# Pre-norm attention and gated feed-forward on one core: the maxima's product, the zero rows, and the order of values, first products and layer norms

## The chip, the cores and the metric

The kernel runs on one core of one Trainium2 chip. A core has five engines with an instruction queue each, which they work through in order: TensorE (PE in the profile; its weight loads are PEld), VectorE (DVE), ScalarE (ACT), GpSimd (POOL) and SyncE (SP), which here issues every DMA. Matrix products are written to PSUM, which has eight banks of 128 x 512 fp32 values; operands lie in SBUF, with 128 partitions. The metric is the device time of one execution in microseconds (us).

## The reference

One transformer block on 2048 tokens of width 448, in fp32. The parts that matter:

```python
def _A_ref(x, wqkv, wo):
    B, S, D = x.shape
    H = 16; Dh = D // H; W = 256
    qkv = (x @ wqkv).reshape(B, S, 3, H, Dh).transpose(2, 0, 3, 1, 4)
    q, k, v = qkv[0], qkv[1], qkv[2]
    scores = jnp.einsum("bhqd,bhkd->bhqk", q, k) * (Dh ** -0.5)
    mask = (idx[:, None] - idx[None, :] >= 0) & (idx[:, None] - idx[None, :] < W)
    scores = jnp.where(mask[None, None], scores, -1e9)
    p = _softmax(scores, axis=-1)
    o = jnp.einsum("bhqk,bhkd->bhqd", p, v)
    return o.transpose(0, 2, 1, 3).reshape(B, S, D) @ wo
...
h = x + _A_ref(_layernorm(x), A_wqkv, A_wo)
h2 = h + _B_ref(_layernorm(h), B_w_gate, B_w_up, B_w_down)   # (gelu(x@gate) * (x@up)) @ down, 1792 wide
```

A query sees itself and the 255 tokens before it. There are 16 heads of 28 columns.

## The kernel before

**Numbers.** Operands of products are split in a high part (fp32r, rounded by an ACT copy, `to_hi`, L349) and a low part (the rest, by a DVE subtraction, `to_lo`, L352). A product x @ w is the sum of high x high, low x high and high x low: 11 matmuls (`TERMS`) for the 448 rows of the contraction, which are held as four row blocks.

**Layer norm** (`layer_norm`, L364). For each tile of 128 tokens: statistics on DVE (L369, L372), three small steps on POOL that make scale and offset (L376 to L378), the normalising copy on ACT (L382), four fp32 transposes on TensorE against `ident` (L386), and high and low parts into `xT`. There are 16 tiles in the first norm and 16 in the second.

**Attention.** It runs in 16 blocks B: two halves p of the heads, in each four chunks c of 512 tokens, in each two groups of four heads. `project` makes q and k of a group for a chunk (L526); they go to DRAM and come back re-arranged (`put`, `loads`), q into `rq`, k into `rk`. Both have two halves u, used by even and odd blocks. `values` makes v of the half (L492). In a block, `scores` (L575) computes 16 score products, and DVE takes each row's masked maximum (L579). `maxima` (L587) splits the negated maxima of four heads in high and low parts, eight columns `mhl`; TensorE turns them by a transpose (L603), and ACT writes them into rows 96 to 103 of `rq` (`put`, L605). `probs` (L642) is the product of k and q with 104 contraction rows: rows 0 to 83 hold the three parts of q and k, rows 84 to 95 are zeros, rows 96 to 103 the maxima on the q side and a 0/1 pattern that picks the head's own on the k side. So the maximum is subtracted within the product, and ACT only takes the exponential (L646). POOL cuts the triangles off (`select`, L657), TensorE multiplies by v in fp32 (`attend`, L676), the sums are turned and divided (`drain`), and `output` multiplies by wo and adds to the residual `hres` (L714, L717).

The zeros are written by POOL (`zeros`, L462, eight memsets at L469, after the first layer norms' POOL steps), the pattern by DVE (eight copies at L456).

**Feed-forward.** 56 products: 14 column groups of 128 by four token chunks. Each is 22 gate and up matmuls (L801), gelu on ACT (L810), the multiplication on DVE (L813), high and low parts, and 12 down matmuls (L820). Weights are staged in `raw` or in the memory of v and split into high and low parts (`weights`, L746). The activation buffer `ge` is one tile of its own.

**The order.** The kernel records every operation with an engine, a cost, a latency, a key and what it reads and writes (`Lists.op`, L73). A planner (`run`, L150) then plays the engines forward: at each step an engine takes, among the operations that could start about soonest, the one with the lowest key. That gives the fixed order in which each engine's queue is filled; where two operations need a PSUM bank, `allowed` (L887) says which banks a kind may have. Keys are in units of one sixteenth of a block; the feed-forward part has keys from 1000 on. DMAs have a planned place on SP in the same way. In the first 26 us of the plan `idle` (L907) fills TensorE's gaps with transposes of `ident` (L913).

Of the kernel before, what the change touches and what calls it, by code (L numbers as in the profile page):

```python
# [20 lines left out]
EPS = 1e-5  # L21
# [17 lines left out]
FFN = 1000  # L39
SPANS = {"pp", "proj", "raw", "xT", "h", "rqf", "rkf", "vm", "rec0", "rec1", "rec2"}  # L40
# [9 lines left out]
def mm(n):  # L50
    return n / 2400 + 0.0155
# [14 lines left out]
class Lists:  # L66
# [42 lines left out]
    def plan(self, allowed, idle, rounds):  # L109


        best = None
        for i in range(rounds):
            end = self.run(allowed, idle, False)
            if end is not None and (best is None or end < best[0]):
                best = (end, [o.key for o in self.ops])
            if end is None or i == rounds - 1:
                break
            self.latest(end)
        for o, key in zip(self.ops, best[1]):  # L120
            o.key = key

    def latest(self, end):


        at = {o: i for i, o in enumerate(self.order)}
        back, cand = {}, {}
        for o in self.ops:
            o.left, o.ready = len(o.users), end
            if not o.left:  # L130
                cand.setdefault(o.eng, []).append(o)
        n = len(self.ops)
        while n:
            best = None
            for e, l in cand.items():
                for o in l:
                    t = min(back.get(e, end) - o.cost, o.ready - (o.fin - o.start))
                    if best is None or (t, at[o]) > best[0]:
                        best = ((t, at[o]), o)
            (t, _), o = best  # L140
            cand[o.eng].remove(o)
            o.key = back[o.eng] = t
            n -= 1
            for d in o.deps:
                d.left -= 1
                d.ready = min(d.ready, t + d.fin - d.start - d.cost if d.eng == o.eng == "pe" else t - WAKE[o.eng])
                if not d.left:
                    cand.setdefault(d.eng, []).append(d)

    def run(self, allowed, idle, emit=True):  # L150
# [49 lines left out]
        while n:  # L200
# [5 lines left out]
            if best is None:  # L206
                return None
            t, o, got = best
            e = o.eng
            if e == "pe" and t > free["pe"] + 0.1:  # L210
                cost = idle(free["pe"], t, bank_free, emit)
                if cost:
                    free["pe"] += cost
                    continue
# [17 lines left out]
            if emit:  # L232
                o.fn()
# [16 lines left out]
def block_kernel(ctx: ExitStack, tc, x, wqk_in, wv_in, wo_in, ffn_in, out):  # L250
# [24 lines left out]
    ge = pool.tile([128, 512], F32, name="ge")  # L275

    pool.tile([128, 16], F32, name="pad")
    nhalf = pool.tile([128, 1], F32, name="nhalf")
    e8 = pool.tile([128, 8], F32, name="e8")
    bnst = [pool.tile([128, 6], F32, name=f"bnst{i}") for i in range(2)]  # L280
    bnmv = [pool.tile([128, 2], F32, name=f"bnmv{i}") for i in range(4)]
    bnve = [pool.tile([128, 3], F32, name=f"bnve{i}") for i in range(4)]
    mx = [pool.tile([128, 4], F32, name=f"mx{i}") for i in range(4)]
    mhl = [pool.tile([128, 8], F32R, name=f"mhl{i}") for i in range(3)]
# [21 lines left out]
    rq = rq_m.rearrange("p (u j t) -> p u j t", u=2, j=4)  # L306
    rk = rk_m.rearrange("p (u j t) -> p u j t", u=2, j=4)
    pp = pp_m.rearrange("p (j t) -> p j t", j=4)
    v = v_m.rearrange("p (t g h d) -> p t g h d", t=NT, g=2, h=4)
    mask = mt[:, 0:384]  # L310
    junk = [mt[:, 384 + 192 * i:576 + 192 * i].bitcast(BF) for i in range(2)]
# [7 lines left out]
    def span(name, lo, n):  # L319
        return (name, lo, lo + n)  # L320
# [24 lines left out]
    def V(t):  # L345
        return span("vm", t, 1)
# [17 lines left out]
    def layer_norm(t, key, kind):  # L364
# [3 lines left out]
        def stats():  # L368
            nc.vector.bn_stats(bnst[i2], hres[:, t, :])  # L369

        def aggr():
            nc.vector.bn_aggr(bnmv[i4], bnst[i2])  # L372

        def ve():
            mv, e = bnmv[i4], bnve[i4]
            nc.gpsimd.tensor_scalar(e[:, 0:1], mv[:, 1:2], EPS, None, op0=OP.add)  # L376
            nc.gpsimd.tensor_tensor(e[:, 1:2], e[:, 0:1], nhalf, op=OP.pow)
            nc.gpsimd.tensor_scalar(e[:, 2:3], mv[:, 0:1], e[:, 1:2], -1.0, op0=OP.mult, op1=OP.mult)  # L378

        def norm():  # L380
            e = bnve[i4]
            nc.scalar.activation(xn[i2], hres[:, t, :], AF.Identity, scale=e[:, 1:2], bias=e[:, 2:3])  # L382
# [15 lines left out]
        op("dve", 0.65, 0.63, key, stats, [HR(t)], [("bnst", i2)])  # L398
        op("dve", 0.1, 0.195, key, aggr, [("bnst", i2)], [("bnmv", i4)])
        op("pool", 1.25, 1.3, key, ve, [("bnmv", i4), "nhalf"], [("bnve", i4)], port=True, tag="ve")  # L400
        op("act", 0.54, 0.63, key, norm, [HR(t), ("bnve", i4)], [("xn", i2)])
# [7 lines left out]
    def start():  # L409
# [43 lines left out]
        op("pool", 0.85, 0.9, -30, const_pick, (), ["e8"], port=True)  # L453
        for u in range(2):
            for j in range(4):
                op("dve", 0.55, 0.54, -24 + 8 * u + 2 * j, lambda u=u, j=j: nc.vector.tensor_copy(  # L456
                    rk[96:104, u, j], e8[96:104, j:j + 1].to_broadcast([8, 768])), ["e8"], [("pick", u, j)], port=True)
# [3 lines left out]

    def zeros():  # L462

        after = [o for o in L.ops if o.tag == "ve"]
        for u in range(2):
            for m, w, n in ((rq_m, "zq", 2048), (rk_m, "zk", 3072)):
                for i in range(2):
                    op("pool", 0.1 + 0.5 * n * 0.00081, 0.15 + 0.5 * n * 0.00081, -36 + 8 * u + i,
                       lambda m=m, n=n, u=u, i=i: nc.gpsimd.memset(  # L469
                           f(m[64:96, (2 * u + i) * n // 2:(2 * u + i + 1) * n // 2]), 0.0), (), [(w, u, i)],  # L470
                       after=after)
# [15 lines left out]
    def values(p, t):  # L487
        key = 128 * p + 8 * t - (37 if t < 4 and not p else 24)
# [59 lines left out]
    def loads(B):  # L548
# [3 lines left out]
        def get(s, cc, lo, n, at, key):  # L552
# [5 lines left out]
            dma(key, 246 * n, lambda: nc.sync.dma_start(f(dst[0:3 * DH, u, :, at * 128:(at + n) * 128]), src),  # L558
# [8 lines left out]
    def scores(B, i, j):  # L567
# [6 lines left out]
        def one():  # L574
            nc.tensor.matmul(bank[b.k][:, o:384], rq[0:3 * DH, u, j, i * 128:i * 128 + 128],  # L575
                             rk[0:3 * DH, u, j, m0 * 128:(i + 3) * 128], start=True, stop=True)
# [4 lines left out]
        op("pe", mm(384 - o), 0.19 + (384 - o) / 2400, s, one, [("rq", u, i)] + [("rk", u, m) for m in range(m0, i + 3)],  # L581
# [5 lines left out]
    def maxima(B, i):  # L587
# [13 lines left out]

        def tr():
            nc.tensor.transpose(bank[b.k][0:8, 384:512], f(m), ident)  # L603

        def put():  # L605
            to_hi(rq[96:104, u, :, i * 128:i * 128 + 128],
                  bank[b.k][0:8, None, 384:512].to_broadcast([8, 4, 128]))
        op("pe", 0.11, 0.286, key, tr, [("mh", k), ("ml", k), "ident"], (), b)
# [25 lines left out]
    def probs(B, m, j, o):  # L634
# [6 lines left out]
        def one():  # L641
            nc.tensor.matmul(bank[b.k][:, 0:n], rk[0:104, u, j, m * 128:m * 128 + 128],  # L642
                             rq[0:104, u, j, lo * 128:(hi + 1) * 128], start=True, stop=True)
# [102 lines left out]
    def weights(i, key):  # L746
# [3 lines left out]
        if q:  # L750
            raw, at0, need = v_m[:, 1472 * (q - 1):1472 * q], 1472 * q, ["vfree"]
# [215 lines left out]
```

## Time and profile before

| | |
|---|---|
| median of three runs | 776.94 us (774.67 to 777.94) |
| profiled execution | 777.91 us |
| its span, first to last instruction | 775.9 us |
| mean granted TensorE clock | 0.991 |
| TensorE busy | 753.0 us, 97% |
| VectorE, ScalarE, GpSimd busy | 408.0, 332.0, 176.3 us |
| DMA | 70.48 MB, 29.5% of 16 engines on SP's queue |
| first matmul; first scores | 7.6 us; 42.7 us |
| full feed-forward products | from 372 us on, 7.47 us each |
| last matmul ends | about 770.5 us |

Busy time of TensorE counts a matmul from its start to its modelled end, and matmuls overlap: the time from one matmul's start to the next one's tells more of the rate (0.23 us for 512 columns). PEclk, the granted clock, is 1 at full speed.

### The profile page before, as it was taken

To read this page: it belongs to the slowest core of one execution; us is meant where nothing else is said; L and a number is where in the kernel's file an instruction comes from. 1 tells how busy PE (TensorE), PEld (TensorE's weight loads), DVE (VectorE), ACT (ScalarE), POOL (GpSimd) and SP (SyncE) were. 2 spreads that over 40 slices of the span, in tenths; PEclk is the share of its full clock that TensorE was granted. 3 is DMA by queue.
4 is the path that set the end of the run, shared out by engine and by line. 5 is a ranking of instruction groups with operands and counts; after the bars stand their busy time and mean duration, and the time that the engine had idled before them with its cause. 6 is when DMAs were issued, how large, how long until landed. Compare 5 with 4: busy or idle time off the path is not lost.

```text
span 775.9 us, 11718 instructions
## 1 busy us (share of the span) xinstructions
PE 753.0 (97%) x4282; PEld 622.4 (80%) x4282; DVE 408.0 (53%) x1106; ACT 332.0 (43%) x727; POOL 176.3 (23%) x283
## 2 busy tenths in 40 slices
PE   6799999999999999999999999999999999999997
PEld 5687788878878776777888888888888888888885
DVE  7887966776677879857513344222242322223232
ACT  4476857776667778686211232111231111111111
POOL 7724334244335457555000000000000000000000
PEclk9899999999999999899999999999999999999999
DMA  8697446765565465223400021000000000001111
GB/s 279 188 295 217 135 132 189 193 175 160 159 188 156 119 171 170 76 80 97 138 1 1 0 79 39 1 1 1 0 1 1 0 1 1 0 1 48 47 48 47
DMA packets 44401, 70.48 MB, mean 91 GB/s; under 512 B 3832, under 2 KB 34488, under 8 KB 44344
## 3 DMA queue, kind: packets, MB, share of 16 engines
q1 hardware_dynamic: 44344, 69.75, 29.5%
q8 instruction: 33, 0.54, 0.3%
q14 instruction: 24, 0.20, 0.1%
HBM read 44.04 MB, written 25.69 MB: 90 GB/s over the span
## 4 chain that ended last, share of the span: by engine, by line
PE 88%; DVE 4%; POOL 2%; ACT 2%; DMA 2%; issue 1%; SPq 0%; DVEq 0%; POOLq 0%; ACTq 0%
PE bank L801 35%; PE bank L820 17%; PE bank L526 9%; PE bank L642 6%; PE bank L575 5%; PE bank L676 5%; PE bank L714 5%; PE bank L492 4%; DVE mt L579 1%; PE bank L386 1%; PE bank L603 1%; DMA rk<-k 1%; POOL rk L469 1%; DMA hres<-in_x_dram 1%; DVE xT L352 1%
## 5 line engine op out<-in xcount | busy, mean ns | idle before, releaser
L813 DVE TENSOR_TENSOR ge<-bank,ge 128x512 f32<-128x512 f32 x56 | 38.7, 691 | 214.1 <-PE bank L801 212.9
L579 DVE CUSTOM_DVE_ANT_0 mt<-bank,mt 128x384 bf16<-128x384 f32 (+2 forms) x256 | 129.1, 526 | 39.3 <-PE bank L575 36.9
L646 ACT ACTIVATE pp<-bank 128x384 f32<-128x384 f32 (+2 forms) x352 | 126.7, 390 | 48.5 <-PE bank L642 41.3
L526 PE MATMUL bank<-xT,proj 128*128 128x512 f32 x308 | 106.2, 417 | 4.4 <-DVE proj L352 4.3
L349 ACT ACTIVATE proj<-ge 128x512 fp32r<-128x512 f32 x56 | 35.4, 632 | 165.8 <-DVE ge L813 165.8
L657 POOL TENSOR_SCALAR_AFFINE_SELECT pp<-pp 128x512 f32<-128x512 f32 x120 | 75.0, 638 | 132.5 <-ACT pp L646 129.8
L642 PE MATMUL bank<-rq,rk 104*128 104x384 f32 (+2 forms) x352 | 101.5, 310 | 2.1 <-ACT pp L646 1.3
L810 ACT ACTIVATE ge<-bank 128x512 f32<-128x512 f32 x56 | 33.6, 599 | 151.3 <-PE bank L801 149.7
L801 PE MATMUL bank<-xT,proj 128*128 128x512 f32 x352 | 91.1, 392 | 0.3 <-ACT pp L646 0.3
L801 PE MATMUL bank<-xT,rec 128*128 128x512 f32 x352 | 91.0, 395 | 0.0
L801 PE MATMUL bank<-xT,rk 128*128 128x512 f32 x352 | 90.1, 391 | 0.0
L575 PE MATMUL bank<-rk,rq 84*128 84x384 f32 (+2 forms) x256 | 84.6, 351 | 0.9 <-DMA rk<-k 0.3
L642 PEld LDWEIGHTS bank<-rq,rk 104*128 104x128 f32 x352 | 66.4, 192 | 20.0 <-ACT pp L646 5.7
L801 PEld LDWEIGHTS bank<-xT,rec 128*128 128x128 f32 x352 | 66.1, 188 | 13.5
L801 PEld LDWEIGHTS bank<-xT,rk 128*128 128x128 f32 x352 | 66.1, 188 | 12.4
L801 PEld LDWEIGHTS bank<-xT,proj 128*128 128x128 f32 x352 | 65.8, 188 | 12.5 <-ACT pp L646 0.4
L526 PEld LDWEIGHTS bank<-xT,proj 128*128 128x128 f32 x308 | 57.7, 196 | 12.7 <-issue 4.6
L492 PE MATMUL bank<-proj,xT 128*128 128x224 f32 x352 | 56.7, 281 | 0.2 <-DVE xT L352 0.2
L352 DVE TENSOR_TENSOR proj<-ge,proj 128x512 fp32r<-128x512 f32 x56 | 38.7, 691 | 33.6 <-ACT proj L349 33.0
L575 PEld LDWEIGHTS bank<-rk,rq 84*128 84x128 f32 x256 | 47.5, 192 | 10.5 <-DVE mx L579 3.5
L492 PEld LDWEIGHTS bank<-proj,xT 128*128 128x128 f32 x352 | 50.9, 192 | 1.7 <-issue 0.4
L714 PE MATMUL bank<-wos,ohl 128*128 128x448 f32 x192 | 50.4, 375 | 1.1 <-ACT ohl L349 0.8
(81 smaller groups left out, 1034.1 us busy)
## 6 DMA issues: line engine op xcount, KB each, us to landing
rk<-k SPq DMA_DIRECT2D x44, 336.0 KB
rq<-q SPq DMA_DIRECT2D x32, 336.0 KB
q<-proj SPq DMA_DIRECT2D x16, 448.0 KB
v<-in_ffn_dram SPq DMA_DIRECT2D x8, 736.0 KB
k<-proj SPq DMA_DIRECT2D x12, 448.0 KB
raw<-in_ffn_dram SPq DMA_DIRECT2D x6, 736.0 KB
hres<-in_x_dram SPq DMA_DIRECT2D x16, 224.0 KB
q<-proj SPq DMA_DIRECT2D x16, 224.0 KB
```

Source lines behind the costliest of these rows:

```text
L352: (eng or nc.vector).tensor_sub(dst, src, f(hi))
L492: op("pe", mm(224), 0.29, key + a / 16, lambda a=a, h=h, wb=wb, xb=xb: nc.tensor.matmul(bank[b.k][:, 0:224], xT[:, xb, t * 128:(t + 1) * 1 ...
L526: op("pe", mm(512) + 0.002, 0.403, key, lambda a=a, h=h, wb=wb, xb=xb: nc.tensor.matmul(bank[b.k], wqk[i][:, h, wb, :], xT[:, xb, c * 512: ...
L575: nc.tensor.matmul(bank[b.k][:, o:384], rq[0:3 * DH, u, j, i * 128:i * 128 + 128], rk[0:3 * DH, u, j, m0 * 128:(i + 3) * 128], start=True, ...
L579: nc.vector.tensor_tensor_reduce(junk[s % 2][:, o:384], bank[b.k][:, o:384], mask[:, o:384], 1.0, -BIG, OP.add, OP.max, mx[i][:, j:j + 1])
L642: nc.tensor.matmul(bank[b.k][:, 0:n], rk[0:104, u, j, m * 128:m * 128 + 128], rq[0:104, u, j, lo * 128:(hi + 1) * 128], start=True, stop=True)
L646: nc.scalar.activation(pp[:, j, o * 128:o * 128 + n], bank[b.k][:, 0:n], AF.Exp, scale=SCALE)
L657: nc.gpsimd.affine_select(a, a, pattern=[[0, 4], [-cm, 128]], compare_op=op_, fill=0.0, base=0, channel_multiplier=cm)
L676: nc.tensor.matmul(bank[b.k][32 * j:32 * j + DH + 1, lo * 128:(hi + 1) * 128], v[:, 4 * c - 2 + m, g % 2, j, :], pp[:, j, at[m] * 128:(at[ ...
L714: op("pe", mm(D), 0.38, wk, lambda a=a, h=h, oh=oh, wh=wh, i=i, k=k: nc.tensor.matmul(bank[k.k][:, 0:D], ohl[:, h, oh, i * 128:(i + 1) * 1 ...
L801: op("pe", mm(512), 0.403, key + q * NP + a / NP, lambda a=a, h=h, wb=wb, xb=xb, q=q, b=b: nc.tensor.matmul(bank[b.k], get()[0][q][h][:, w ...
L820: op("pe", mm(D), 0.38, key + 2 * NP + 3 * q + a, lambda a=a, oh=oh, wh=wh, q=q, b=b: nc.tensor.matmul(bank[b.k][:, 0:D], gh(oh)[:, q, :], ...
```

## The change

Five things are changed, and with them the order of all engines, since the planner is run on the new list.

1. **Maxima.** `mhl` is 96 columns wide and zero but for the first eight. An ordinary fp32r product of its first 72 columns with an fp32r unit matrix `one_r` takes the transpose's place; rows 0 to 7 of its result are used as before. The plan's cost of a matmul gets a floor of 0.115 us.
2. **Zero and pick rows.** For u = 0 they are written at the very start: zeros by three DVE memsets and one ACT copy, the pattern by two DVE and two ACT copies. For u = 1 rows 84 to 103 of `rk` and 84 to 95 of `rq` are copied from u = 0 by two DMAs on SP. `zeros` and its POOL memsets are gone.
3. **Values of the second half** have keys 12 units higher (three quarters of a block later).
4. **Early products.** The 44 gate and up matmuls of products 0 and 1 (`EARLY = 2`) may run in the attention part, on bank 6 or on those that scores and probabilities no longer need, once projections and values are done. ACT copies the results into the memory of v; gelu and multiplication read them there, after the last exponential as before. `ge` now lies in the mask's tile.
5. **Layer norms.** The POOL steps are done for two tiles at once, in four instructions and not two times three (tiles 0 and 1 stay alone). The second norm of tiles 4 to 15 is given keys in the feed-forward part, at 60 units before the product that has the tile's number; it may use banks 0 to 3 there.

The wait on v's memory for staged weights is now kept per range and not for all of v. The planner's second pass, which was not in use, is gone.

```diff
-    return n / 2400 + 0.0155
+    return max(n / 2400 + 0.0155, 0.115)
...
-    def layer_norm(t, key, kind):
+    def layer_norms(ts, key, kind):
+        i, n = ts[0] % 4, len(ts)
+        def ve():
+            e = bnve[:, :, i:i + n]
+            nc.gpsimd.tensor_scalar(e[:, 0], bnmv[:, i:i + n, 1], EPS, None, op0=OP.add)
+            nc.gpsimd.tensor_tensor(e[:, 1], e[:, 0], nhalf[:, 0:n], op=OP.pow)
+            if n == 1:
+                nc.gpsimd.tensor_scalar(e[:, 2], bnmv[:, i:i + n, 0], e[:, 1], -1.0, op0=OP.mult, op1=OP.mult)
+            else:
+                nc.gpsimd.tensor_tensor(e[:, 0], bnmv[:, i:i + n, 0], e[:, 1], op=OP.mult)
+                nc.gpsimd.tensor_scalar(e[:, 2], e[:, 0], -1.0, None, op0=OP.mult)
...
-        for u in range(2):
-            for j in range(4):
-                op("dve", 0.55, 0.54, -24 + 8 * u + 2 * j, lambda u=u, j=j: nc.vector.tensor_copy(
-                    rk[96:104, u, j], e8[96:104, j:j + 1].to_broadcast([8, 768])), ["e8"], [("pick", u, j)], port=True)
+        op("act", 0.2, 0.3, -99, lambda: to_hi(one_r, ident), ["ident"], ["one"])
+        for i in range(2):
+            op("dve", 1.1, 1.15, -99 + i, lambda i=i: nc.vector.memset(f(rq_m[64:96, 1024 * i:1024 * i + 1024]), 0.0),
+               (), [("zq", 0, i)])
+        op("dve", 1.65, 1.7, -97, lambda: nc.vector.memset(f(rk_m[64:96, 0:1536]), 0.0), (), [("zk", 0, 0)])
+        op("act", 1.45, 1.55, -97, lambda: nc.scalar.activation(
+            rk_m[64:96, 1536:3072], e8[64:96, 0:1].to_broadcast([32, 1536]), AF.Copy), ["e8"], [("zk", 0, 1)])
+        for j in range(4):
...
+        dma(-20, 246, lambda: nc.sync.dma_start(f(rk_m[84:104, 3072:6144]), f(rk_m[84:104, 0:3072])),
+            [*(("pick", 0, j) for j in range(4)), *(("zk", 0, i) for i in range(2))],
+            [*(("pick", 1, j) for j in range(4)), *(("zk", 1, i) for i in range(2))])
+        dma(-20, 98, lambda: nc.sync.dma_start(f(rq_m[84:96, 2048:4096]), f(rq_m[84:96, 0:2048])),
...
-        key = 128 * p + 8 * t - (37 if t < 4 and not p else 24)
+        key = 128 * p + 8 * t - ((37 if t < 4 else 24) if not p else 12)
...
         def tr():
-            nc.tensor.transpose(bank[b.k][0:8, 384:512], f(m), ident)
+            nc.tensor.matmul(bank[b.k][0:72, 384:512], m[:, 0:72], one_r,
+                             start=True, stop=True)
...
+        early = n < EARLY
         for q in range(2):
-            b = Bank(("ffn", len(row)))
-            row.append(b)
+            b = Bank("early") if early else Bank(("ffn", len(row)))
...
+        for q, b in enumerate(bs if early else ()):
+            op("act", 0.49, 0.605, 16 * NB - 20, lambda q=q, b=b: nc.scalar.activation(raw[q], bank[b.k], AF.Copy), (),
+               held[q], b)
...
-                for t in range(4 * c, 4 * c + 4):
-                    layer_norm(t, 16 * (8 + 2 * c + 1) + LAG_P + ORDER[5] + LAG_V + 9 + t % 4, "ln2")
+                for i in (0, 2):
+                    layer_norms(range(4 * c + i, 4 * c + i + 2), lambda t: 16 * 9 + LAG_P + ORDER[5] + LAG_V + 9 + t % 4
+                                if t < 4 else FFN + 30 * t - 60, "ln2")
...
+        if kind == "early":
+            return [] if left["proj"] or left["v"] else [6] + ([] if left["score"] else [0, 1]) + \
+                ([] if left["prob"] else [2, 3])
```

More of the change, by code (lines that the diff above doesn't have):

```diff
@@ L107, in fresh, with run @@
         return self.open[tag] == len(self.all[tag])
[L109 to L150, printed above, removed]
+    def run(self, allowed, idle):
         E = ("py", "pe", "dve", "act", "pool", "sp")
```

136 lines of the change are left out of this document (70 added, 66 removed).

## The prediction

> **What bounds the kernel now.** I read the page's busy shares, its slices and its chain first. TensorE is the bound: busy for 97% of the span and 88% of the chain that ended last.
>
> ```profile
> PE 753.0 (97%) x4282; PEld 622.4 (80%) x4282; DVE 408.0 (53%) x1106; ACT 332.0 (43%) x727; POOL 176.3 (23%) x283
> ...
> PE   6799999999999999999999999999999999999997
> PEclk9899999999999999899999999999999999999999
> ...
> PE 88%; DVE 4%; POOL 2%; ACT 2%; DMA 2%; issue 1%; SPq 0%; DVEq 0%; POOLq 0%; ACTq 0%
> ```
>
> A change can therefore gain only where TensorE waits, runs at a reduced clock, or has a dearer instruction than it needs. Two digits of PEclk below 9 say where to look. The second view is busy time by stretch (length, then busy time and count for PE, PEld, DVE, ACT, POOL; then granted clock, DMA share, GB/s):
>
> ```profile
> 16.50:24.20 7.70, 5.35 (x26) 4.21 (x24) 7.61 (x7) 2.70 (x5) 7.53 (x7) 1.00 0.26 85
> 24.20:31.10 6.90, 5.74 (x15) 4.62 (x16) 5.72 (x15) 1.26 (x3) 5.76 (x14) 0.51 0.63 185
> 31.10:40.00 8.90, 8.08 (x62) 7.36 (x61) 7.37 (x18) 6.85 (x13) 4.68 (x14) 1.00 0.90 273
> 40.00:290.00 250.00, 247.82 (x1805) 201.01 (x1804) 190.21 (x680) 173.99 (x425) 99.64 (x146) 1.00 0.60 176
> ...
> 297.30:304.10 6.80, 5.84 (x50) 3.69 (x47) 6.38 (x20) 6.57 (x14) 2.47 (x6) 1.00 0.68 205
> 304.10:311.00 6.90, 6.62 (x48) 4.32 (x48) 6.73 (x27) 6.51 (x19) 6.78 (x9) 1.00 0.38 101
> 311.00:317.80 6.80, 6.80 (x41) 4.21 (x40) 4.10 (x14) 3.60 (x11) 2.77 (x5) 0.50 0.72 212
> ...
> 372.00:767.00 395.00, 395.00 (x1792) 334.86 (x1792) 119.61 (x186) 76.01 (x125) 0.00 (x0) 1.00 0.05 18
> ```
>
> The feed-forward part (372 to 767) is full, at 7.47 us a product, and has nothing to give. Weak are 16 to 40 and 297 to 318; each holds 6.8 us at half clock. For the first, the timeline gives the cause:
>
> ```profile
> 3.44 0.63 DVE L369 BATCH_NORM_STATS2 bnst<-hres 128x6 f32<-128x448 f32 x1
> 4.32 0.56 DVE L456 CAST rk<-e 8x768 fp32r<-8x768 f32 x1
> ...
> 16.33 5.48 DVE L456 CAST rk<-e 8x768 fp32r<-8x768 f32 x4
> ...
> 24.52 0.69 DVE L352 TENSOR_TENSOR proj<-bank,proj 128x512 fp32r<-128x512 f32 x1
> ...
> 25.36 1.62 PE L526 MATMUL bank<-xT,proj 128*128 128x512 f32 x3 [3.50 <-DVE proj L352]
> ```
>
> Four pick copies take 1.37 us each, where one alone took 0.56, while POOL writes zeros (L469, 12.5 to 23). The low half that frees a PSUM bank stands behind them on DVE, and TensorE waits 3.5 us for it.
>
> **The change part by part.** The sum is made against the profiled execution, 777.91 us (span 775.9 and 2.0 around it). It stands 1.0 above the median of 776.94; the three runs go from 774.67 to 777.94.
>
> *Zero and pick rows first.* Between 16.5 and 40 TensorE is idle for 2.35 + 1.16 + 0.82 = 4.3 us, and its 5.74 busy us at clock 0.51 cost 2.8 more: 7.1. The POOL memsets and six of eight picks on DVE leave this stretch (four go to a copy by DMA, two to ACT), so the bank is freed as its product ends. What is late next is the start: DVE now has three memsets and two picks ahead of the first statistics, which started at 3.44. At the rate of its bank memset (512 columns in 0.48) the 3,584 columns take 3.4 us, the picks 1.1; from 0.8 this is 5.3, so statistics, POOL's three steps (4.38 to 5.98) and the norm come about 1 us later than 6.79. ACT's extra rows (1,536, two times 768, 128 columns; a 512-column one took 0.59) end near 5.5, before the 6.30 at which the value weights release it. I charge 1.3 and take +5.8; ends +2 (only the wait goes, and the start is later by 1.5) and +7.1.
>
> *Two copies of 344 KB on SP*, ahead of one output-weight load and the first q store. SP is free then (15.4 to 19.9) and the DMA share is 0.26; at 252 GB/s for a share of 0.77 they take about 1.1 us of all engines. First read in block 1, after 45: 0. Without that cover: on one of 16 engines, at the 20 GB/s that this makes for each, 17 us, and the q stores behind them would be 10 late.
>
> *Early products, v later.* From 297.3 to 317.8 the rows hold 20 scores, 27 probability products, 72 attend matmuls, 12 transposes and 5 maxima. At their undisturbed rates (0.18; 0.12 mean; 1.43 per 24; 0.11; 0.105) this is 3.6 + 3.2 + 4.3 + 1.3 + 0.5 = 12.9 us of work in 20.5: 7.6 lost. 3.4 is the half clock (6.80 us, full of work); 4.2 is waiting, for DVE and ACT, which are busy 6.38 and 6.57 of 6.80. The new order puts work there that needs neither at once: 22 of the 44 gate and up matmuls of products 0 and 1 more than before ahead of the last output rows, and 11 more v matmuls after the last projection: 22 x 0.229 + 11 x 0.111 = 6.3 us. That is more than 4.2, but it adds two ACT copies (0.6 each), and not every gap fits. I take 3.0 of the 4.2 and 3.0 of the 3.4: +6.0; ends +1 and +7.6.
>
> The Trainium skill bears on the second number (TensorE: Matmul & The Clock Gate, "Part 1: The HAM clock gate"): the clock halves after an idle window of about 3.4 us. The first stretch agrees (a 3.50 us wait); the second does not, since the longest wait of TensorE on record from 296 to 332 is this (total, times, longest):
>
> ```profile
> PE bank L642 <- ACT pp L646: 0.8, 2, 0.6
> ```
>
> By the rows thin work is enough, so denser work removes it; by the page there is no idle window to remove.
>
> *Maxima product.* Today, from the timeline:
>
> ```profile
> 112.00 0.33 PE L575 MATMUL bank<-rk,rq 84*128 84x384 f32 x1
> 112.17 0.27 PE L603 MATMUL bank<-ident,mhl 128*8 128x128 f32 x1
> 112.20 0.48 PE L526 MATMUL bank<-xT,proj 128*128 128x512 f32 x1
> 112.51 0.34 PE L642 MATMUL bank<-rq,rk 104*128 104x384 f32 x1
> ```
>
> 0.51 us from score to probability product, of which 0.175 + 0.23 are the score's and the projection's: 0.105 for the transpose. A 128-column probability product takes 0.06 (67.00 to 67.06). 64 x 0.045 = +2.9. Ends: +4.9, if only the 0.028 that its start shows remains, and -3.5, if the weights, 72 columns and not 8, are not covered (between 0.085 and 0.188 us by the PEld rows, so 0.055 more). I take the nearest row, the same type and length. The page above gives 0.06 us for 72 weight columns ("LDWEIGHTS"), which no run here shows yet; by it the load hides and the sum is the same.
>
> *Layer norms.* Pairs save POOL steps: 0, POOL is at 23%. Second norms of tiles 4 to 15 move into or next to the feed-forward part, where DVE is busy 120 of 395. A product's high half must be ready within eight gate matmuls (1.83 us); multiply and copy take 0.69 + 0.63, so 0.5 is free, and a norm's ACT pieces (0.76, 0.60) or DVE pieces (0.86) can overrun it a little: -0.5 in all; ends +1 (no second norms at the head, where TensorE waited 0.4) and -4.5, nine tiles at 0.5.
>
> *The joint.* The last exponentials free ACT; then the gelu table (1.28) and product 2's high half come before the next gate matmuls: some 1.3 us of waiting, against 1.4 there now. 0. The stretch 40 to 290 keeps its work in another order: 0, ends -2 and +2.
>
> Sum: 5.8 + 6.0 + 2.9 - 0.5 = 14.2. 777.9 - 14.2 = 763.7, and 0.5 less for a profiled run above its median: **763.2 us**.
>
> **The rivals.**
> 1. *The half clock stays or moves.* It fell at 311 without a long wait, so it may fall elsewhere: 763.2 + 3.0 = 766. For it: nothing on the rows shows the exact condition, and the page's rule asks for an idle window that is not there. Against it: it falls only in the two thinnest stretches.
> 2. *The gaps don't fill.* At 297 to 311 DVE and ACT are at 94 to 98%; if their pace holds TensorE's order up all the same, that term shrinks to its lower end, +1: 768. For it: in-order engines, and the copies added. Against it: the filler stands between the waiting instructions.
> 3. *Slower: norms inside the feed-forward part.* If each of nine late tiles holds a product up by its whole chain (transpose 0.44, norm 0.76, copy 0.60, low half 0.86: 2.66 us), 24 us come back: 787. It decides from (13.7 + 3.9) / 9 = 2.0 us per tile on. Against it: each engine's order there leaves 0.5 us free per product and places the pieces between two products.
> 4. *The product gains nothing* (weights not covered): 763.2 + 6.4 = 769.6.
>
> **How the numbers follow.** Forecast 0.55 (757 to 766), rival 1 0.13, rival 2 0.13, rival 4 0.07, rival 3 0.06; 0.06 for a start or a copy that is late by ten and ends near 774. 0.5% of 776.94 is 3.9 us, about what a measurement can tell from no change: faster means below 773.1. The first, second, and fourth rivals lie below it: 0.87 faster, with 0.06 the same and 0.07 slower. The range takes the forecast's gains from half to full and reaches to rivals 1, 2 and 4: 756.5 to 773.5.
>
> **What would show it.** PE's 3.5 us wait on the low half gone, and no PEclk digit below 9 between 16 and 40; first score matmuls near 37 and not 42.7. Gate matmuls among the scores near 290 to 320, PEclk full there. The maxima row 0.06 from its start to the end of its effect. Attention over about 13 us sooner, products still 7.47. Wrong it is if DVE waits before the first norm cost over 3 us, if PEclk dips in other slices, or if products with a norm beside them last 8 us and more.

## The result, and the profile after

The changed kernel takes 772.89 us (median of 20 runs, 770.82 to 776.67) where the kernel before takes 777.34 (20 runs, 774.11 to 778.71): a ratio of the mean times of **0.9952** (95% interval 0.9938 to 0.9966). It is faster by some 4 us; 13.7 were forecast. The profiled execution of the changed kernel took 775.56 us, 2.7 above its median, with a span of 773.8.

The first view is the page, its parts on busy time, slices and chain:

```profile
PE 748.5 (97%) x4280; PEld 624.2 (81%) x4280; DVE 404.3 (52%) x1103; ACT 337.3 (44%) x735; POOL 154.8 (20%) x248
...
PE   5999999999999999999999999999999999999996
...
PEclk9999999999999999999999999999999999999999
...
PE 85%; DMA 6%; DVE 4%; ACT 3%; issue 1%; POOL 0%; DVEq 0%; SPq 0%; ACTq 0%
```

TensorE still bounds, and both dips of the granted clock are gone from the slices. The second is busy time by stretch (length, then busy time and count for PE, PEld, DVE, ACT, POOL; then granted clock, DMA share, GB/s):

```profile
16.50:24.20 7.70, 7.70 (x45) 6.45 (x44) 7.27 (x19) 4.42 (x9) 4.40 (x12) 1.00 0.62 149
24.20:31.10 6.90, 6.90 (x43) 6.04 (x42) 4.97 (x12) 2.01 (x6) 2.12 (x3) 1.00 0.86 282
31.10:40.00 8.90, 7.76 (x53) 6.70 (x52) 5.58 (x14) 7.32 (x14) 3.83 (x9) 1.00 1.02 278
40.00:290.00 250.00, 246.20 (x1783) 201.41 (x1782) 187.21 (x679) 172.39 (x421) 95.08 (x134) 0.99 0.59 173
...
297.30:304.10 6.80, 6.15 (x53) 5.81 (x56) 5.84 (x22) 6.03 (x15) 4.61 (x9) 1.00 0.84 261
304.10:311.00 6.90, 6.26 (x50) 4.44 (x42) 5.33 (x12) 6.22 (x18) 6.82 (x8) 1.00 0.62 162
311.00:317.80 6.80, 6.80 (x55) 5.77 (x48) 5.92 (x25) 4.96 (x13) 3.48 (x6) 1.00 0.52 156
...
372.00:767.00 395.00, 391.90 (x1783) 330.83 (x1782) 122.10 (x194) 81.05 (x134) 1.29 (x3) 1.00 0.04 14
```

Both weak stretches are mended: 24.2 to 31.1 holds 43 matmuls at full clock, not 15 at 0.51, and 311 to 317.8 holds 55, not 41. But 40 to 290 has 22 matmuls fewer than before, and a clock of 0.99. The feed-forward part is no longer full: 391.9 of 395.

Because overlapping matmuls hide waits in busy time, I also worked out the time lost, an estimate: the length of a stretch, less every matmul that starts in it at its undisturbed start-to-start rate (0.23 us for 512 columns, 0.203 for 448, 0.178 for 384, 0.12 for 256, 0.063 and 0.11 for 128, and so on; the same rates for all kernels). The last two columns are profiles from further down: the changed kernel in an execution that had no half clock (called undisturbed below), and the best version found, whose execution had one half clock of 3.4 us at 35.

| stretch, us | before | after | after, no half clock | best version |
|---|---|---|---|---|
| 0 to 40 | 16.4 | 13.3 | 12.5 | 15.4 |
| 40 to 140 | 7.8 | 9.5 | 9.6 | 8.1 |
| 140 to 290 | 12.6 | 14.2 | 12.4 | 12.3 |
| 290 to 318 | 8.4 | 3.5 | 3.0 | 2.7 |
| 318 to 372 | 6.4 | 5.6 | 4.6 | 3.0 |
| 372 to 450 | -0.1 | 2.9 | 2.9 | 0.2 |
| 450 to the end | 7.9 | 8.4 | 8.4 | 8.5 |
| sum | 59.3 | 57.4 | 53.4 | 50.3 |

Before to after: +3.1 at the start, +4.9 at 290 to 318, +0.8 at the joint; and -1.8, -1.6 (a half clock of 3.4 us at 150), -3.1 in the first products, -0.5 in the rest.

The start, first DVE's timeline and then PE's (start, length, engine, line, operation, count, and in brackets the idle time before it):

```profile
2.13 0.91 DVE L427 MEMSET rq<- 32x1024 f32 x1 [0.16 <-issue]
3.31 1.34 DVE L429 MEMSET rk<- 32x1536 f32 x1 [0.27 <-issue]
4.67 1.03 DVE L435 CAST rk<-e 8x768 fp32r<-8x768 f32 x2
5.72 0.63 DVE L338 BATCH_NORM_STATS2 bnst<-hres 128x6 f32<-128x448 f32 x1
```

```profile
8.78 1.12 PE L357 MATMUL bank<-ident,xn 128*128 128x128 f32 x4 [8.78 <-ACT xn L352]
9.69 3.41 PE L907 MATMUL bank<-ident 128*128 128x128 f32 x15
12.89 1.06 PE L357 MATMUL bank<-ident,xn 128*128 128x128 f32 x4
```

The first statistics start at 5.72 and not 3.44, the first transposes at 8.78 and not 7.59. That is about the 1.3 us that I charged. Behind it, 15 idle transposes (L907) take 3.41 us, 0.21 each from start to start, because the clock is full only from 13.9 (before: from 10.6). Most of this second delay is chance. The clock changes on a raster of 3.413 us that lies elsewhere in each execution: in all 14 profiles of this case it is full 3.0 to 6.0 us behind the first transpose, 3.0 in the profile before, 5.1 in this one and 3.3 in the undisturbed one (8.79 and 12.06). First scores come at 40.0 (before 42.7, forecast 37).

### The profile page after: what moved, and what is told of

The parts are those of the page before. It is cut to its first block, busy times and chain, and to the rows that moved or that the text cites. A ratio compares the mean times of both kernels' runs of the same rounds, so it can differ in the third digit from the quotient of the medians.

```text
span 773.8 us, 11634 instructions
## 1 busy us (share of the span) xinstructions
PE 748.5 (97%) x4280; PEld 624.2 (81%) x4280; DVE 404.3 (52%) x1103; ACT 337.3 (44%) x735; POOL 154.8 (20%) x248
## 4 chain that ended last, share of the span: by engine, by line
PE 85%; DMA 6%; DVE 4%; ACT 3%; issue 1%; POOL 0%; DVEq 0%; SPq 0%; ACTq 0%
PE bank L783 35%; PE bank L810 17%; PE bank L502 8%; PE bank L622 6%; PE bank L551 5%; PE bank L656 4%; PE bank L694 4%; PE bank L468 4%; DMA rk<-k 2%; PE bank L357 1%; DMA q<-proj 1%; DVE bnst L338 1%; DMA raw<-in_wqk_dram 1%; DMA raw<-in_ffn_dram 1%; ACT proj L308 1%
## 5 line engine op out<-in xcount | busy, mean ns | idle before, releaser
L803 DVE TENSOR_TENSOR mt<-bank,mt 128x512 f32<-128x512 f32 x54 | 37.4, 692 | 208.9 <-PE bank L783 208.9
L622 PE MATMUL bank<-rq,rk 104*128 104x384 f32 (+2 forms) x352 | 99.1, 302 | 0.2
L801 ACT ACTIVATE mt<-bank 128x512 f32<-128x512 f32 x54 | 32.4, 599 | 149.5 <-PE bank L783 149.5
L308 ACT ACTIVATE proj<-mt 128x512 fp32r<-128x512 f32 x56 | 35.3, 630 | 142.3 <-DVE mt L803 142.3
L551 PE MATMUL bank<-rk,rq 84*128 84x384 f32 (+2 forms) x256 | 82.4, 346 | 2.3 <-DMA rk<-k 1.5
L783 PEld LDWEIGHTS bank<-xT,rk 128*128 128x128 f32 x352 | 65.9, 188 | 12.6
L468 PE MATMUL bank<-proj,xT 128*128 128x224 f32 x352 | 59.9, 280 | 1.2 <-DVE proj L311 0.6
L468 PEld LDWEIGHTS bank<-proj,xT 128*128 128x128 f32 x352 | 52.6, 192 | 3.5 <-DVE proj L311 1.1
L311 DVE TENSOR_TENSOR proj<-mt,proj 128x512 fp32r<-128x512 f32 x56 | 39.1, 698 | 30.0 <-ACT proj L308 29.2
L810 PE MATMUL bank<-rk,proj 128*128 128x448 f32 x192 | 47.8, 369 | 2.7 <-ACT proj L308 2.7
```

The costliest lines, as they stand in the source:

```text
L308: nc.scalar.activation(dst, src, AF.Copy)
L311: (eng or nc.vector).tensor_sub(dst, src, f(hi))
L468: op("pe", mm(224), 0.29, key + a / 16, lambda a=a, h=h, wb=wb, xb=xb: nc.tensor.matmul(bank[b.k][:, 0:224], xT[:, xb, t * 128:(t + 1) * 1 ...
L551: nc.tensor.matmul(bank[b.k][:, o:384], rq[u][0:3 * DH, j, i * 128:i * 128 + 128], rk[u][0:3 * DH, j, m0 * 128:(i + 3) * 128], start=True, ...
L622: nc.tensor.matmul(bank[b.k][:, 0:n], rk[u][0:104, j, m * 128:m * 128 + 128], rq[u][0:104, j, lo * 128:(hi + 1) * 128], start=True, stop=True)
L783: op("pe", mm(512), 0.403, key + q * NP + a / NP, lambda a=a, h=h, wb=wb, xb=xb, q=q, b=b: nc.tensor.matmul(bank[b.k], get()[0][q][h][:, w ...
```

## The experiments

Three groups, each on one chip with its own runs of the kernel before. "At full clock" is the mean over the runs of time x granted clock, an estimate of what a TensorE-bound run would take if it were never slowed; the clock is given to a thousandth, which is 0.8 us. For the kernel before it comes out too low, as the section on the changed kernel again shows. A difference between two rows carries both intervals, together some 0.003 or 2 us.

| kernel | ratio to before (95%) | mean clock | at full clock | before: clock, at full clock |
|---|---|---|---|---|
| maxima by transpose again | 0.9931 (0.9911 to 0.9952) | 0.998 | 772.7 | 0.993, 773.5 |
| second norms two products earlier | 0.9929 (0.9910 to 0.9949) | 0.998 | 771.6 | same |
| first statistics before key rows | 0.9982 (0.9967 to 0.9998) | 0.998 | 776.7 | same |
| no early products | 1.0002 (0.9982 to 1.0022) | 0.995 | 774.6 | same |
| late values at the old key | 0.9980 (0.9963 to 0.9997) | 0.999 | 776.4 | 0.992, 773.0 |
| old price for short matmuls | 0.9881 (0.9857 to 0.9905) | 0.998 | 769.4 | same |
| single first norms | 0.9935 (0.9916 to 0.9954) | 0.999 | 772.5 | same |
| before, rows alone | 0.9981 (0.9964 to 0.9998) | 0.994 | 772.4 | same |
| changed kernel again | 0.9943 (0.9922 to 0.9964) | 0.999 | 772.2 | 0.993, 772.2 |
| old price and earlier norms | 0.9866 (0.9842 to 0.9890) | 0.999 | 766.1 | same |
| these and single norms | 0.9913 (0.9889 to 0.9937) | 0.999 | 769.6 | same |
| before, price floor alone | 1.0052 (1.0034 to 1.0069) | 0.991 | 774.7 | same |

### The maxima's product undone

```diff
-            nc.tensor.matmul(bank[b.k][0:72, 384:512], m[:, 0:72], one_r, start=True, stop=True)
+            nc.tensor.transpose(bank[b.k][0:8, 384:512], f(m[:, 0:8]), ident)
```

> The changed kernel with one line put back: the 64 maxima are turned by the transpose again; the order of all instructions stays. Theory now: my price for the product was read from one interval only (its start to the next start). Over two intervals, up to the second instruction behind it, the product costs 0.115 us more than its neighbours' rates alone (median of 58) and the transpose of before 0.120 (median of 54), so the whole is 64 x 0.005 = 0.3 us slower than the changed kernel's 772.9: 772.5 to 774. Rival, my forecast: 64 x 0.045 = 2.9 us slower, 775.8.

Measured: 0.9931; the changed kernel has 0.9952 and 0.9943. The transpose is not slower by anything that can be seen; 2.9 us more would have made 0.998 to 0.999, outside the interval. So this part of the change is worth nothing that these runs can tell. The reason stands in the timeline of the changed kernel:

```profile
109.96 0.34 PE L551 MATMUL bank<-rk,rq 84*128 84x384 f32 x1
110.13 0.23 PE L582 MATMUL bank<-one,mhl 128*72 128x128 f32 x1
110.19 0.45 PE L502 MATMUL bank<-xT,proj 128*128 128x512 f32 x1
110.48 0.34 PE L622 MATMUL bank<-rq,rk 104*128 104x384 f32 x1
```

From score to probability product it is 0.52 us, and in the kernel before it was 0.51 (112.00 to 112.51). The next start does come 0.06 after the product (0.03 after a transpose), but the one after that is late: 0.29 from projection to probability product, where 0.23 is the rate. Over both intervals a short matmul between long ones costs 0.11 to 0.12 us (medians), whether it is a maxima product, a transpose or a 128-column probability product. What is late is a weight load, in the same timeline's PEld rows:

```profile
110.14 0.19 PEld L502 LDWEIGHTS bank<-xT,proj 128*128 128x128 f32 x1
110.25 0.19 PEld L622 LDWEIGHTS bank<-rq,rk 104*128 104x128 f32 x1
```

The projection's load starts with the short product (110.13), the probability product's load 0.11 later; it ends at 110.44, and its matmul starts at 110.48. The Trainium skill ("TensorE: Matmul & The Clock Gate", section "Back-to-back issue gap") says that in a stream of loads and matmuls the spacing is set by both. The trace agrees, though its 0.11 to 0.12 us is more than the Trainium skill's 0.081 for 128 columns.

### Second norms two products earlier

```diff
-                                if t < 4 else FFN + 30 * t - 60, "ln2")
+                                if t < 4 else FFN + 30 * t - 120, "ln2")
```

> The changed kernel with the second norms' keys two products earlier (FFN + 30 * t - 120 and not - 60). Theory: the feed-forward loss is not nine tiles overrunning a spare 0.5 us but two places (400 and 433 us) where the first product of a new block of 512 tokens needs the tiles that are normed just then, so its gate matmuls can't cover the wait for the product before it; with norms two products ahead both waits (0.93 + 0.19 us each) go: 772.9 - 2.2 = 770.7. Rival: a norm's pieces hold up a product wherever they stand (0.5 us each, as I forecast); then the waits only move to other products and the time stays within 0.7 of 772.9.

Measured: 0.9929, about 1.1 to 1.8 us faster than the changed kernel, an interval that does not exclude zero, and 0.0002 below the run with transposes on the same chip; the traces are clearer. First the place in the changed kernel, its timeline around 400 us:

```profile
399.16 1.03 PE L357 MATMUL bank<-ident,xn 128*128 128x128 f32 x8
399.43 0.69 DVE L803 TENSOR_TENSOR mt<-bank,mt 128x512 f32<-128x512 f32 x1 [5.17 <-PE bank L783]
399.79 0.60 ACT L308 ACTIVATE xT<-bank 128x512 fp32r<-128x512 f32 x1 [2.99 <-PE bank L357]
400.29 0.62 ACT L308 ACTIVATE proj<-mt 128x512 fp32r<-128x512 f32 x1
...
400.96 0.67 PE L810 MATMUL bank<-rk,proj 128*128 128x448 f32 x2 [0.77 <-ACT proj L308]
```

Usually the next product's gate matmuls cover multiplication and high part (0.69 + 0.62). Here the next product is the first of a new token chunk, and its `xT` is what these eight transposes only begin to make. So the planner had nothing to put in between, and ACT besides made `xT` first. It happens once per chunk: at 367, 400 and 433. Then this line of PE's waits in the changed kernel (total, times, longest), and its busy time from 372 to 450:

```profile
PE bank L810 <- ACT proj L308: 4.2, 4, 1.5
```

```profile
372.00:450.00 78.00, 76.42 (x357) 64.10 (x356) 27.12 (x47) 21.32 (x36) 1.29 (x3) 1.00 0.02 5
```

and the same in the experiment:

```profile
PE bank L810 <- ACT proj L308: 1.8, 2, 1.5
```

```profile
372.00:450.00 78.00, 78.00 (x369) 66.39 (x368) 29.75 (x51) 22.60 (x38) 1.30 (x3) 1.00 0.06 20
```

In both kernels seven tiles' transposes lie in these 78 us; here the stretch is full again, with 12 matmuls more. The 1.5 us left are the wait of the very last product. So norms between products cost next to nothing here; one whose output the next product needs makes TensorE wait, 0.77 to 1.16 us at each of the three places. The runs show less of this than the profiles. At the start, where all engines have the same order as in the changed kernel, this profile lost 2.4 us to a late transfer and a half clock (last section); how often the other runs did is not known.

### First statistics ahead of part of the rows

```diff
-        op("dve", 1.65, 1.7, -97, lambda: nc.vector.memset(f(rk_m[64:96, 0:1536]), 0.0), (), [("zk", 0, 0)])
+    def rows():
+        op("dve", 1.65, 1.7, -39.5, lambda: nc.vector.memset(f(rk_m[64:96, 0:1536]), 0.0), [("bnmv", 0)], [("zk", 0, 0)])
```

The function is called behind the first tile's norm, and makes the two DVE picks and the two DMA copies too.

> The changed kernel with DVE's part of key rows and picks (one memset, two copies) behind the first tile's statistics. Theory: these are what delays the first norm (7.96 against 6.79 us before), and by that the full clock (from 13.9 and not 10.6 us): transposes start near 6.6 and not 8.8 us, the full clock comes one step of 3.4 us sooner, and 2 to 3 us go: 770 to 771. Rival: the second tile's rows arrive at 6.9 us all the same and bound the next norm, the gap is filled with idle transposes, and the time stays at 772.9 within 0.7.

Measured: 0.9982, 2.3 to 3.0 us slower than the changed kernel, so both expectations missed. The cause that I named is right as far as it goes: transposes start at 7.52 and the clock is full at 11.9. But the planner made another order of it, with 58 idle transposes and not 20; 23 of them in a row take 4.37 us and stand ahead of real work, and the norms of tiles 2 and 3 come later. Without idle transposes the matmuls started by 40 us are worth 22.7 us here and 24.5 in the changed kernel. What a start with the earlier norm and the old order would bring was not tried.

### Early products left out, and late values undone

```diff
-EARLY = 2
+EARLY = 0
```

> The changed kernel without the early products (EARLY = 0), v's second half still late. Theory: the early gate and up matmuls close the gaps between 290 and 318, where the changed kernel lost 3.5 us and the one before 8.4; without them half of the 4.9 us comes back, and the half clock may: 775 to 778. Rival: the later v matmuls do it alone, or the two ACT copies and the four held values cost what the filler brings: 772 to 773.5.

Measured: 1.0002. The early products are worth 3.9 to 4.6 us beside the changed kernel's two ratios (5.5 beside the run with transposes, on the same chip). The stretches of this run:

```profile
297.30:304.10 6.80, 6.18 (x56) 4.75 (x54) 5.75 (x19) 6.06 (x15) 6.47 (x11) 1.00 0.64 219
304.10:311.00 6.90, 5.93 (x25) 4.12 (x29) 3.49 (x12) 5.03 (x17) 3.77 (x6) 0.59 1.00 291
311.00:317.80 6.80, 6.30 (x44) 3.99 (x36) 5.25 (x21) 5.53 (x13) 3.05 (x5) 0.91 0.43 128
```

The half clock is back (0.59), 25 matmuls stand where the changed kernel has 50, and the mean clock of the runs falls from 0.998 to 0.995. The other half of that step:

```diff
-        key = 128 * p + 8 * t - ((37 if t < 4 else 24) if not p else 12)
+        key = 128 * p + 8 * t - ((37 if t < 4 else 24) if not p else 24)
```

> The changed kernel (0.9952 of the time before) with the value products of the second half at their old key (-24 and not -12); the early products stay. Forecast's theory: 11 value matmuls are filler at the end, 1.2 us; without them 0.9952 + 0.0015 = 0.997, and the loss between 290 and 318 rises from 3.5 to about 5 us. Rival: the early products alone fill that stretch, and late values only push work about in the middle: 0.994 to 0.9955, the loss at 290 to 318 as it was.

Measured: 0.9980, so the late values are worth 2.2 to 2.9 us, twice the filler that I counted, and not where I put it. The clock stays (0.999). In its profile the loss between 290 and 318 is 3.8; 2.8 us more than in the undisturbed profile of the changed kernel are lost at 318 to 372, and 2.0 at 140 to 290.

### The planner's price

```diff
-    return max(n / 2400 + 0.0155, 0.115)
+    return n / 2400 + 0.0155
```

> The changed kernel with the planner's old price for short matmuls (n / 2400 + 0.0155, no floor of 0.115 us); the instructions are the same, the order is another. Between 40 and 140 us the changed kernel loses 9.5 us of TensorE's time beyond its rates, in all five profiles that have this order (9.5 to 9.8), where the one before loses 7.75. Theory: it is the floor, which makes the planner count 0.05 us too many at some 180 short matmuls, so that transposes and copies are put where their input is late (1.05 us at 73.5): without it the loss falls to 8 or less and the time to 0.993. Rival: the paired norms do it; then the loss stays at 9.5 and the time at 0.995.

Measured: 0.9881, 4.8 to 5.5 us faster than the changed kernel (0.9943 and 0.9952), five runs. Its profile shows little of that, for it is of the slowest of the five (776.39; the others 768.42 to 770.90), with 10.2 us at half clock: the loss from 40 to 140 is 8.3 us (9.5 with the floor). One of the waits that go is this, from the changed kernel's timeline:

```profile
73.24 0.77 ACT L352 ACTIVATE xn<-hres,bnve 128x448 f32<-128x448 f32 x1
...
73.52 0.25 PE L582 MATMUL bank<-one,mhl 128*72 128x128 f32 x1
74.04 0.58 ACT L308 ACTIVATE rq<-bank 8x512 fp32r<-8x512 f32 x1
...
74.67 0.28 PE L582 MATMUL bank<-one,mhl 128*72 128x128 f32 x1 [0.91 <-ACT rq L308]
```

Two maxima products stand one behind the other, and the second waits until ACT, after a norm, has emptied the first's bank. Another stands near 149: with the floor the second half's projection weights are split from 138.7 on, ACT waits 5.1 us for their loads, and TensorE waits 0.7 and 0.8 for DVE, ahead of the half clock at 150; without it the split starts at 132.1, and these waits are gone. The rival for the same stretch was the paired norms:

```diff
-                for i, n in ((0, 1), (1, 1), (2, 2)) if c == 0 else ((0, 2), (2, 2)):
+                for i, n in ((0, 1), (1, 1), (2, 1), (3, 1)):
```

> The changed kernel with the first layer norms one tile at a time, as before; second norms stay in pairs. Theory (rival of the run on costs): two norms of 0.76 us back to back on ACT hold up the copy that frees the maxima's bank (73.2 to 74.7 us), and 2 us are lost so between 40 and 140; single norms bring the loss there from 9.5 to 8 and the time to 0.993. Rival: the planner's floor does it, and this run stays at 9.5 us and 0.995.

Measured: 0.9935, not to be told from the changed kernel; the loss from 40 to 140 is 7.7 us, but 140 to 290 has 13.7, where the undisturbed profile of the changed kernel has 12.4. So another order mends that stretch too, and gives it back elsewhere. To see whether the floor or one unlucky order is at fault, it was put alone into the kernel before:

```diff
-    return n / 2400 + 0.0155
+    return max(n / 2400 + 0.0155, 0.115)
```

> The kernel before with the planner's floor of 0.115 us for short matmuls and nothing else: the same instructions in another order. Theory: the floor itself misplaces work, whatever the kernel, and costs here what it cost in the changed kernel: +2 to +5 us, 1.003 to 1.007. Rival: it is not the floor but the one order that came of it; another order may fall out as well or as badly, and this run lies within 0.003 of 1, or below it.

Measured: 1.0052, 4.0 us slower with the same instructions but for two idle transposes fewer. Its loss is not in the stretch that I had expected: 40 to 140 is better (6.7 against 7.8), while 140 to 290, 290 to 318 and 318 to 372 lose 1.8, 1.7 and 1.7 more. So in both kernels the order with the floor is the worse one, by 4.0 and by 4.8 to 5.5 us. How it comes about is open: the price itself is right for a short matmul between long ones (0.11 to 0.12 measured, above). In this planner a truer price did not make a better order.

### The rows alone

On the kernel before, steps one and two of the forecast (zero and pick rows first, two copies) and nothing else:

```diff
+        op("pool", 0.85, 0.9, -100.5, const_pick, (), ["e8"], port=True)
+        for i in range(2):
+            op("dve", 1.1, 1.15, -99 + i, lambda i=i: nc.vector.memset(f(rq_m[64:96, 1024 * i:1024 * i + 1024]), 0.0),
+               (), [("zq", 0, i)])
...
-                    zeros()
```

> The kernel before with nothing but zero and pick rows written first and copied (steps one and two of the forecast). Forecast: +5.8 us, 0.9925. Theory now: the wait of 3.5 us and the half clock at 24 go (6.0 us), but the start is late by 1.2 us and the clock gets full one step of 3.4 us later, so that 3.3 us more real work is done by 40, and 0.9957. Rival: what is won by 40 is waited for later, since blocks in the middle are bound by other engines as well: 0.999 to 1.001.

Measured: 0.9981, 1.5 us, less than either number; the rival's 0.999 lies within the interval. Its profile does have the wait and the half clock gone: from 16.5 to 31.1 it loses 0.2 us where the kernel before lost 6.2. Against that it loses 1.6 more before 16.5 and 0.9 more from 31.1 to 40. That leaves 3.5 us between these two executions (777.91 and 774.50), more than the runs show: one profile is not the mean. Over all runs the mean clock went from 0.9923 to 0.9939, which is 1.3 us at most and not the 3.4 that 6.8 us at half speed would cost.

### The changed kernel again, and the best version

> The changed kernel unaltered, on the chip of the next three runs, with the granted clock of each run of both kernels. Every theory: 0.994 to 0.9965. Theory on where the gain lies: it is mostly clock. From the runs of the kernel before (mean granted clock 0.9926, so 5.7 us lost) and of the changed one (0.9984, 1.2 us lost), 4.5 us of the gain are clock and under 1.5 us are the rest. Rival: half or more of the gain remains once each run's time is multiplied by its clock.

Measured: 0.9943. The kernel before has 0.9928 of the clock, 5.6 us lost by this reckoning; the changed one 0.9989, 0.9 us lost. Time x clock is 772.2 us for both, which would make all of the net gain clock. But the runs of the kernel before don't bear that reckoning out. In the three groups (64 runs) their time falls by 0.34 to 0.41 us for each 0.001 of clock, where time x clock takes 0.78 for granted; the changed kernel's falls by 1.0. At 0.37 us, the slope of all 64 runs (95% interval 0.24 to 0.50), the 0.006 of clock is worth 2.3 us, **about half of the net gain**; the rest would then be waits. At full price it would be all of it, which the slope speaks against. The split is an estimate from runs whose half clocks fell by chance, and no run settles it.

Then the edits that helped, together, and with single norms as a third:

> The changed kernel with two edits together: the planner's old price for short matmuls, and second norms two products earlier. Theory: they act in different stretches (40 to 300; 366 to 435) and add up: 0.9881 - 0.0023 = 0.986, range 0.983 to 0.989. Rival: the 0.9881 of the first edit came from five lucky runs (its profile's own run was 776.4), its real worth is the 1.7 us that was expected of it, and both together give 0.990 to 0.992.

> As the run before it, with single first norms as a third edit. Theory: alone they gave 0.9935 (0.0017 below the changed kernel), with most of it in the same 40 to 140 that the old price mends as well, so little is left: 0.984 to 0.987. Rival: pairs were made for another order, and single norms cost POOL and ACT time here: 0.988 or more.

The first gives 0.9866: 767.22 us beside 777.72, faster than both kernels. The two edits add up, as far as intervals of 0.002 can tell. From the page and the stretches of its profile:

```profile
PE 748.2 (98%) x4282; PEld 625.6 (82%) x4282; DVE 399.4 (52%) x1103; ACT 336.4 (44%) x735; POOL 156.4 (20%) x248
```

```profile
297.30:304.10 6.80, 6.80 (x60) 5.55 (x59) 5.43 (x22) 6.70 (x17) 6.47 (x11) 1.00 0.47 147
304.10:311.00 6.90, 6.90 (x60) 5.57 (x59) 5.43 (x17) 5.69 (x19) 4.78 (x6) 1.00 0.68 182
311.00:317.80 6.80, 6.80 (x50) 4.37 (x48) 6.75 (x27) 6.53 (x15) 5.40 (x7) 1.00 0.14 56
```

Sixty matmuls and no wait where the kernel before has 50 and 48. Single norms on top cost some 3 us (0.9913): what helped a little in one order harmed the other.

## Why the prediction was wrong, step by step

Sign and range held (faster, 756.5 to 773.5), but the forecast of 763.2 was 9.7 us too low. By its own terms:

- **Zero and pick rows, +5.8: mis-sized.** 1.5 us by the run that has them alone. The 3.5 us wait and the half clock at 24 went as I said, and the 1.3 us charged for a later start were 2.2 (after), 1.3 (undisturbed) and 1.6 (rows alone) up to 16.5. What failed is the size of the gain. 31.1 to 40 loses 0.2 to 0.9 more, where I counted its 0.8 us of idle time as won. And I took one profile's 6.8 us of half clock, at its full price of 2.8, for the mean: the mean clock rose by 0.0016 only, and by the runs of the kernel before 6.8 us of half clock (0.0044 of the clock) go with 1.6 us.
- **Copies, 0: right.** No wait in the first blocks names them.
- **Early products and late values, +6.0: right.** Between 290 and 318 the loss fell by 4.9 (5.4 in the undisturbed profile), half clock included; the runs price the two edits at 3.9 to 4.6 and 2.2 to 2.9. The sizes within were off: values 2.2 and more, not 1.2, and largely after 318 and before 290. The filler itself is as counted: 22 gate and up matmuls and 11 more v matmuls lie between 290 and 318.
- **Maxima product, +2.9: failed.** Measured 0. The step that fails is the price of 0.06, read from "67.00 to 67.06": one interval, while for the transpose I had taken both. Read alike, 128-column products cost 0.11 to 0.12 as well. The product's own load of 72 columns, for which I had 0.06, takes 0.14 us in the PEld rows (109.96). Rival 4 had the heading, "gains nothing", but its price of 6.4 us is that of a loss of 3.5; 2.9 are missing.
- **Second norms, -0.5: mis-sized and mis-explained.** -3.1 in the profile from 372 to 450, which earlier keys undo; by the runs that undoing is worth 0.1 to 1.8. "Eight gate matmuls" as cover was the error: at the first product of a chunk they wait for the norm themselves. Rival 3 had the mechanism, but for nine tiles and not at three places.
- **The stretch 40 to 290, 0: failed.** It lost 3.4 us more in the profile, 1.7 of them a half clock at 150; and as most of the 64 maxima lie there, I had some 2 us of gain in it. The prediction has no term for the floor in the planner's price; alone it costs 4.0 us, undone it gives 4.8 to 5.5. With the rows this is the largest of the steps that failed.
- **The joint, 0:** +0.8 (1.8 undisturbed), in the kernel's favour.

Rows (4.3 us too high), maxima (2.9), norms (up to 2.6) and the floor (4.0 to 5.5) make 11 to 15 us, more than the 9.7 that are missing; the late values (1.0 to 1.7 more than forecast) and the joint (0.8) stand against them. The single prices come from edits that each change the order of all the rest, so they need not add up. That the time still fell into the range is therefore partly luck.

Of the signs that I named, the wait is gone, PEclk is full at 16 to 40 and at 311, and gate matmuls stand among the scores (from 305.6 on); a half clock at 150, a maxima product that costs 0.11 to 0.12 and not 0.06, first scores at 40 and products that wait at 367, 400 and 433 were the signs against.

## What to carry to other kernels

Price a short instruction over the start of the second one behind it, and read the old and the new one in the same way; one start-to-start interval can make the same 0.12 us look like 0.03 or 0.06. When cover is counted ("the next product's matmuls hide it"), ask at each boundary of the loops whether the cover itself needs what is being made. And where an order is computed, every number that feeds the planner is a change to all stretches: try it alone, and compare many runs, each time beside its clock, since one profile can hold a half clock that others lack. Time x clock does not by itself tell what the clock cost: here the kernel before followed it by half only.

## What the runs showed of the hardware

**The half clock sits on a free raster.** In 14 profiles all changes of the granted clock lie 3.413 us or multiples of it apart, at another offset in each execution. Counting the matmuls of each full-clock step from 10 us on at their undisturbed rates: every step that was filled to under 0.41 was followed by a half-clock step (nine of nine), some of those between 0.41 and 0.53 were (five), and none above. One from the run with all three edits (stretches as above):

```profile
29.11:32.52 3.41, 3.33 (x28) 3.05 (x26) 0.69 (x1) 0.32 (x2) 0.00 (x0) 1.00 0.96 231
32.52:35.94 3.42, 0.93 (x7) 0.77 (x7) 2.26 (x5) 3.42 (x8) 1.74 (x3) 1.00 1.04 214
35.94:39.35 3.41, 3.41 (x19) 3.41 (x18) 2.14 (x6) 2.26 (x5) 2.70 (x9) 0.50 1.03 274
```

Nine of the 14 half clocks lasted one step, five lasted two. So a gap that falls into one step can halve the next, and cut in two by the raster it can pass: the changed kernel's gap near 147 left a step 0.52 full in one profile, and a half clock followed; in the undisturbed one the emptiest step there was 0.66 full, and none did. A small delay is enough. In the run with earlier second norms all engines have the changed kernel's order up to 313 us, but one store landed later; first the changed kernel, then that run:

```profile
32.01 0.60 ACT L308 ACTIVATE proj<-bank 128x512 fp32r<-128x512 f32 x1 [0.34 <-DMA k<-proj]
32.80 0.60 ACT L308 ACTIVATE proj<-bank 128x512 fp32r<-128x512 f32 x1 [1.15 <-DMA k<-proj]
```

TensorE's wait behind it grew from 0.6 to 1.4 us, the step was 0.26 full and not 0.45, a half clock followed at 34.8, and the first scores came at 42.5 and not 40.0. That fits the spread of one kernel's runs (4.4 to 9 us where there are 12 or more), and clock and time go together in the changed kernel's 20 runs (correlation -0.8). The Trainium skill ("TensorE: Matmul & The Clock Gate", "Part 1: The HAM clock gate") gives a free-running window of 3413 ns, and the trace agrees; but it asks for an idle window, and none of these 14 steps was idle, not even beside the 3.5 us wait of the kernel before (0.24): they were 0.14 to 0.53 full.
